# Linear attention over 32 heads: the last head's q work in halves, wide warm-up products, and new hand-written orders

## The chip, the cores and the metric

The kernel runs on one core of a Trainium2 chip. The metric is the time of one execution on the device, in microseconds (us). A core has a matrix engine (PE), a vector engine (DVE), a scalar engine (ACT), a general engine (POOL) and a sync engine (SP), which here only issues DMA transfers. Sixteen DMA engines carry the transfers.

## The reference

Every head has q, k and v of 2048 rows by 128 columns, in bf16.

```python
B, H, S, D = 1, 32, 2048, 128
phi_q = jnp.where(q > 0, q + 1, jnp.exp(q)) + 1e-6
phi_k = jnp.where(k > 0, k + 1, jnp.exp(k)) + 1e-6
kv  = jnp.einsum("bhsd,bhse->bhde", phi_k, v)
z   = jnp.einsum("bhsd->bhd", phi_k)
num = jnp.einsum("bhqd,bhde->bhqe", phi_q, kv)
den = jnp.einsum("bhqd,bhd->bhq", phi_q, z)[..., None] + 1e-6
return num / den
```

The feature map is computed as min(exp(x), 1) + 1e-6 plus max(x, 0). The two parts go through the products separately and are added in the accumulator.

## The kernel before

A head's 2048 rows are 16 tiles of 128 rows. The work of head h is cut into named operations, and each name carries the head and a part number:

- `ldk`, `ldq`, `ldv`: loads of 512 KB on SP's queue (line 300). Head 0's are two halves of 256 KB. There are 7 buffers for each of k, q and v (`NI`), so a load waits until the head 7 before has used its buffer.
- `ek` (ACT, line 312): exp of k. `em` (DVE, line 315): min and add. `rkd` (DVE, line 318) and `rkp` (POOL, line 322): max(k, 0), eight tiles each. `v1` (POOL, line 326): copies v beside a column of ones, so that z comes out of the same product.
- `kv` (PE, line 333): 32 products into one accumulator, in two halves of 16. `kvs` (ACT, line 338) copies the result to bf16.
- `T` (PE, line 344): 16 transposes of q into the one buffer `xT`. `eq` (ACT, line 347): exp of `xT`. `emq` (DVE, line 349): min and add. `rqa` (ACT, line 353) and `rqb` (DVE, line 356): max(q, 0), eight tiles each.
- `n` (PE, lines 363, 368 and 370): the numerator and denominator products, in two groups (12 and 4 tiles; for head 31 three groups of 6, 6 and 4). `r` (DVE, line 377): reciprocal of the denominators. `f` (DVE, line 384): the final product into one of 12 output buffers (`NO`).
- `st` (SP, line 392): the store, 512 KB; head 31's goes in pieces of 192, 192 and 128 KB. `f` of head h waits for the store of head h - 12.
- `w0`, `w1`, `w2` (PE, line 291): products on the identity matrix that nobody reads. They keep PE busy at the start.

Every engine runs its operations in the order that `ORDER` writes out by hand; a semaphore wait is put in wherever an operation needs another engine's result. So an operation that waits holds all that stands behind it on its engine, and a load or store that waits holds all later ones on SP. Waits that matter here: T of a head waits for `eq`, `rqa` and `rqb` of the head before, since `xT` is one buffer; `eq` waits for the `n` of the head two before; `n` of a group waits until `f` of the head before has emptied its banks. `rkp` and `v1` also wait for `f` and `r` of the head three before (`gate`). A half operation waits only for the halves that it touches:

```python
def over(name, h, parts, t0, t1):
    return [f"{name}{h}.{i}" for i, (a, b) in enumerate(parts(h)) if a < t1 and t0 < b]
```

Of the kernel before, what the change touches and what calls it, by code (L numbers as in the profile page):

```python
# [8 lines left out]
ENGINES = ("PE", "DVE", "ACT", "POOL", "SP")  # L9
NH = 32  # L10
NI, NO, NE, NR, NV, NQ, NK = 7, 12, 2, 2, 2, 2, 2
WARM = (60, 15, 15)
HALVES = ((0, 8), (8, 16))
WHOLE = ((0, 16),)

# [2 lines left out]
    return HALVES if h == 0 else WHOLE  # L18


q_parts = v_parts = k_parts


def kv_parts(h):
# [29 lines left out]
def gate(name, h):  # L54
    if h < 3:
# [3 lines left out]

ORDER = {  # L60
    "PE": """
        w2 T0.1 T0.0 w1 w0 T1.0 kv0.0 kv0.1 n0.0 kv1.0 kv1.1 T2.0 n0.1 n1.0 kv2.0 kv2.1 T3.0 n1.1 kv3.0 kv3.1 n2.0
        T4.0 n2.1 kv4.0 kv4.1 n3.0 T5.0 n3.1 kv5.0 kv5.1 n4.0 T6.0 n4.1 kv6.0 kv6.1 n5.0 T7.0 n5.1 kv7.0 kv7.1 n6.0
        T8.0 n6.1 kv8.0 kv8.1 n7.0 T9.0 n7.1 kv9.0 kv9.1 n8.0 T10.0 n8.1 kv10.0 kv10.1 n9.0 T11.0 n9.1 kv11.0 kv11.1
        n10.0 T12.0 n10.1 kv12.0 kv12.1 n11.0 T13.0 n11.1 kv13.0 kv13.1 n12.0 T14.0 n12.1 kv14.0 kv14.1 n13.0 T15.0
# [1 line left out]
        kv18.1 n17.0 T19.0 n17.1 kv19.0 kv19.1 n18.0 T20.0 n18.1 kv20.0 kv20.1 n19.0 T21.0 n19.1 kv21.0 kv21.1 n20.0  # L67
        T22.0 n20.1 kv22.0 kv22.1 n21.0 T23.0 n21.1 kv23.0 kv23.1 n22.0 T24.0 n22.1 kv24.0 kv24.1 n23.0 T25.0 n23.1
        kv25.0 kv25.1 n24.0 T26.0 n24.1 kv26.0 kv26.1 n25.0 T27.0 n25.1 kv27.0 kv27.1 n26.0 T28.0 n26.1 kv28.0
        kv28.1 n27.0 T29.0 n27.1 kv29.0 kv29.1 n28.0 T30.0 n28.1 kv30.0 kv30.1 n29.0 T31.0 n29.1 kv31.0 kv31.1 n30.0  # L70
        n30.1 n31.0 n31.1 n31.2
    """,
    "DVE": """
        rkd0.0 ones v1ones0 emq0.1 rqb0 emq0.0 rkd1.0 em0.0 em0.1 v1ones1 eps0 eps1 em1.0 eps2 emq1.0 rqb1 r0.0 f0.0
        rkd3.0 rkd2.0 em2.0 em3.0 rqb2 emq2.0 r0.1 f0.1 r1.0 rkd4.0 f1.0 em4.0 rqb3 r1.1 rkd5.0 f1.1 r2.0 emq3.0
        f2.0 em5.0 rqb4 r2.1 rkd6.0 f2.1 r3.0 emq4.0 f3.0 em6.0 rqb5 r3.1 rkd7.0 f3.1 r4.0 emq5.0 f4.0 em7.0 rqb6
        r4.1 f4.1 r5.0 emq6.0 f5.0 em8.0 rqb7 r5.1 f5.1 rkd8.0 r6.0 emq7.0 f6.0 em9.0 rqb8 r6.1 f6.1 rkd10.0 rkd9.0
        r7.0 emq8.0 f7.0 rkd11.0 rqb9 r7.1 em10.0 f7.1 r8.0 emq9.0 f8.0 em11.0 rqb10 r8.1 f8.1 rkd12.0 r9.0 emq10.0
        f9.0 em12.0 r9.1 rqb11 f9.1 emq11.0 r10.0 rkd13.0 f10.0 em13.0 rqb12 r10.1 f10.1 rkd14.0 r11.0 emq12.0 f11.0
        em14.0 r11.1 rqb13 f11.1 rkd15.0 r12.0 emq13.0 f12.0 em15.0 r12.1 rqb14 f12.1 rkd16.0 r13.0 emq14.0 f13.0  # L80
        em16.0 r13.1 rqb15 f13.1 rkd17.0 r14.0 emq15.0 f14.0 em17.0 r14.1 rqb16 f14.1 rkd18.0 r15.0 emq16.0 f15.0
        em18.0 rqb17 r15.1 rkd19.0 f15.1 r16.0 emq17.0 f16.0 em19.0 rqb18 r16.1 rkd20.0 f16.1 r17.0 emq18.0 f17.0
        em20.0 rqb19 r17.1 rkd21.0 f17.1 r18.0 emq19.0 f18.0 em21.0 rqb20 r18.1 f18.1 rkd22.0 r19.0 emq20.0 f19.0
        em22.0 rqb21 r19.1 f19.1 rkd23.0 r20.0 emq21.0 f20.0 em23.0 rqb22 r20.1 rkd24.0 f20.1 r21.0 emq22.0 f21.0
# [132 lines left out]
def bass_standalone__linear_attn_elu__prompt_kernel(nc: bass.Bass, q: bass.AP, k: bass.AP, v: bass.AP, out: bass.AP):  # L217
# [4 lines left out]
    NC = D + 1  # L222
# [6 lines left out]
    with ExitStack() as es:  # L229
        names = [0]  # L230

        def alloc(make, shape, dt):
            names[0] += 1
            return es.enter_context(make(f"la_{names[0]}", shape, dt))
# [222 lines left out]
```

## Time and profile before

| | us |
|---|---|
| median of 4 runs | 173.5 (172.84 to 173.87) |
| the profiled execution, its own time | 173.3 |
| its span in the profile | 171.4 |
| ACT busy in it | 153.3 |
| PE busy in it | 161.5 |
| DVE busy in it | 155.2 |

Times in the trace count from the start of the span. The line numbers are those of the kernel before. `PEld` is PE's load of the stationary operand, which overlaps its products. A DMA is told by the time from its issue on SP to its landing; it has landed when all 16 DMA engines have finished their part of it. The page cuts the span in 40 slices of 4.3 us; a digit is the busy share in tenths.

### The profile page before, as it was taken

To read this page: it belongs to the slowest core of one execution; us is meant where nothing else is said; L and a number is where in the kernel's file an instruction comes from. 1 tells how busy PE (TensorE), PEld (TensorE's weight loads), DVE (VectorE), ACT (ScalarE), POOL (GpSimd) and SP (SyncE) were. 2 spreads that over 40 slices of the span, in tenths; PEclk is the share of its full clock that TensorE was granted. 3 is DMA by queue.
4 is the path that set the end of the run, shared out by engine and by line. 5 is a ranking of instruction groups with operands and counts; after the bars stand their busy time and mean duration, and the time that the engine had idled before them with its cause. 6 is when DMAs were issued, how large, how long until landed. Compare 5 with 4: busy or idle time off the path is not lost.

```text
span 171.4 us, 6462 instructions
## 1 busy us (share of the span) xinstructions
PE 161.5 (94%) x2842; PEld 158.9 (93%) x2842; DVE 155.2 (91%) x266; ACT 153.3 (89%) x131; POOL 85.2 (50%) x71
## 2 busy tenths in 40 slices
PE   3997999999999999999999999999999999999771
PEld 3997989999999999999999999999999999999770
DVE  0539979999999999999999999999999999999883
ACT  2698799999999999999999999999999999996600
POOL 1255545556654565555665556655555555463000
PEclk9999999999999999999999999999999999999978
DMA  5999999999999999999999999999999999999883
GB/s 160 380 403 414 412 403 404 410 404 420 410 412 407 409 420 410 415 408 404 418 410 410 410 410 419 408 408 418 415 415 420 413 420 414 415 417 416 335 326 135
DMA packets 19180, 67.52 MB, mean 394 GB/s; under 512 B 2129, under 2 KB 2513, under 8 KB 19153
## 3 DMA queue, kind: packets, MB, share of 16 engines
q1 hardware_dynamic: 19152, 67.12, 97.9%
q8 instruction: 22, 0.36, 0.8%
q14 instruction: 6, 0.04, 0.1%
HBM read 50.33 MB, written 16.78 MB: 392 GB/s over the span
## 4 chain that ended last, share of the span: by engine, by line
ACT 58%; PE 29%; DVE 8%; DMA 2%; issue 2%; SPq 0%; DVEq 0%
ACT la L347 23%; ACT la L312 22%; ACT la L353 10%; PE la L333 10%; PE la L368 7%; PE la L370 6%; PE la L344 5%; DVE la L384 4%; ACT la L338 3%; DMA la<-in_q_dram 2%; DVE la L356 1%; DVE la L349 1%; DVE la L315 1%; PE la L363 1%; DVE la L377 1%
## 5 line engine op out<-in xcount | busy, mean ns | idle before, releaser
L384 DVE TENSOR_TENSOR la<-la 128x1536 bf16<-128x1536 f32 (+2 forms) x65 | 77.7, 1197 | 0.7
L370 PE MATMUL la<-la 128*128 128x129 bf16 x512 | 69.3, 222 | 0.0
L368 PE MATMUL la<-la 128*128 128x129 bf16 x512 | 69.2, 221 | 0.0
L347 ACT ACTIVATE la<-la 128x2048 bf16<-128x2048 bf16 (+1 forms) x33 | 60.1, 1825 | 5.9 <-PE la L344 3.7
L333 PE MATMUL la<-la 128*128 128x129 bf16 x1024 | 64.2, 219 | 0.4 <-DVE la L281 0.4
L312 ACT ACTIVATE la<-la 128x2048 bf16<-128x2048 bf16 (+1 forms) x33 | 61.2, 1861 | 0.0
L326 POOL COPY la<-la 128x1024 int32<-128x1024 int32 (+1 forms) x33 | 40.6, 1232 | 41.1 <-DVE la L377 34.7
L333 PEld LDWEIGHTS la<-la 128*128 128x128 bf16 x1024 | 60.1, 97 | 0.6 <-DVE la L281 0.6
L322 POOL TENSOR_SCALAR la<-la 128x1024 bf16<-128x1024 bf16 x32 | 43.9, 1371 | 29.4 <-DVE la L384 24.0
L370 PEld LDWEIGHTS la<-la 128*128 128x128 bf16 x512 | 50.0, 98 | 0.0
L368 PEld LDWEIGHTS la<-la 128*128 128x128 bf16 x512 | 47.7, 98 | 0.0
L344 PE MATMUL la<-la 128*128 128x128 bf16 x512 | 34.6, 222 | 1.6 <-DMA la<-in_q_dram 1.4
L363 PE MATMUL la<-la 128*128 128x3 bf16 (+1 forms) x192 | 32.5, 170 | 2.6 <-DVE la L384 1.9
L353 ACT ACTIVATE la<-la 128x1024 bf16<-128x1024 bf16 x32 | 32.6, 1018 | 0.0
L344 PEld LDWEIGHTS la<-la 128*128 128x128 bf16 x512 | 30.0, 99 | 2.3 <-DMA la<-in_q_dram 1.6
L315 DVE TENSOR_SCALAR la<-la 128x2048 bf16<-128x2048 bf16 (+1 forms) x33 | 23.2, 704 | 2.8 <-ACT la L312 2.8
L356 DVE TENSOR_SCALAR la<-la 128x1024 bf16<-128x1024 bf16 x32 | 21.8, 680 | 2.0 <-ACT la L347 1.3
L349 DVE TENSOR_SCALAR la<-la 128x2048 bf16<-128x2048 bf16 (+1 forms) x33 | 22.2, 672 | 1.4 <-ACT la L347 1.3
L363 PEld LDWEIGHTS la<-la 128*128 128x128 bf16 x192 | 18.9, 99 | 4.1 <-DVE la L384 2.8
L318 DVE TENSOR_SCALAR la<-la 128x1024 bf16<-128x1024 bf16 x32 | 14.2, 448 | 5.3 <-DMA la<-in_k_dram 5.3
L377 DVE RECIPROCAL la<-la 128x12 f32<-128x12 f32 (+2 forms) x65 | 12.8, 198 | 1.3 <-PE la L370 0.6
L338 ACT ACTIVATE la<-la 128x129 bf16<-128x129 f32 x32 | 9.0, 281 | 1.4 <-PE la L333 1.4
(14 smaller groups left out, 15.4 us busy)
## 6 DMA issues: line engine op xcount, KB each, us to landing
la<-in_k_dram SPq DMA_DIRECT2D x31, 512.0 KB, 15.6
la<-in_q_dram SPq DMA_DIRECT2D x31, 512.0 KB, 15.5
la<-in_v_dram SPq DMA_DIRECT2D x31, 512.0 KB, 15.3
out_dram<-la SPq DMA_DIRECT2D x31, 512.0 KB, 15.1
la<-in_q_dram SPq DMA_DIRECT2D x2, 256.0 KB, 3.0
la<-in_k_dram SPq DMA_DIRECT2D x2, 256.0 KB, 4.0
la<-in_v_dram SPq DMA_DIRECT2D x2, 256.0 KB, 6.3
out_dram<-la SPq DMA_DIRECT2D x2, 192.0 KB, 2.2
```

The costliest lines, as they stand in the source:

```text
L312: add("ACT", f"ek{h}.{i}", lambda e, a=a, b=b: e.activation(em_sb[:, h % NE, a:b], k_sb[:, h % NI, a:b], ACT.Exp), [f"ldk{h}.{i}"] + freed ...
L315: add("DVE", f"em{h}.{i}", lambda e, a=a, b=b: e.tensor_scalar(em_sb[:, h % NE, a:b], em_sb[:, h % NE, a:b], 1.0, EPS, op0=ALU.min, op1=AL ...
L322: add("POOL", f"rkp{h}.{i}", lambda e, a=a, b=b: e.tensor_scalar(rk_sb[:, h % NR, a:b], k_sb[:, h % NI, a:b], BIG, 0.0, op0=ALU.min, op1=A ...
L326: add("POOL", f"v1{h}.{i}", lambda e, a=a, b=b: e.tensor_copy(v1_sb[:, h % NV, a:b, 0:D].bitcast(i32), v_sb[:, h % NI, a:b].bitcast(i32)), ...
L333: ins = e.matmul(kv_ps, lhsT=src[:, j], rhs=v1_sb[:, h % NV, j, 0:NC], start=(j + part == 0), stop=(j == NT - 1 and part == 1))
L344: ins = e.transpose(xT[:, j], q_sb[:, h % NI, j], ident[:])
L347: add("ACT", f"eq{h}.{i}", lambda e, a=a, b=b: e.activation(emq_sb[:, h % NQ, a:b], xT[:, a:b], ACT.Exp), [f"T{h}.{i}"] + freed(NQ, h, ("n ...
L353: add("ACT", f"rqa{h}", lambda e: e.activation(rq_sb[:, h % NQ, 0:n], xT[:, 0:n], ACT.Relu), over("T", h, q_parts, 0, n) + freed(NQ, h, (" ...
L363: e.matmul(_ap(o_ps[:, :], o + D, [[NC, m]]), lhsT=ones[:], rhs=epsr[:, 0:m], start=True, stop=False, skip_group_check=True)
L368: e.matmul(to, lhsT=emq_sb[:, h % NQ, t], rhs=kvs_sb[:, h % NK], start=False, stop=False, skip_group_check=True)
L370: ins = e.matmul(to, lhsT=rq_sb[:, h % NQ, t], rhs=kvs_sb[:, h % NK], start=False, stop=True, skip_group_check=True)
L384: return e.tensor_tensor(out=_ap(o_sb[:, :, :, :], first(o_sb[:, h % NO, t0, 0:1]) - first(o_sb[:, :, :, :]), [[m * D, nb], [D, m], [1, D] ...
```

## The change

- q of head 31 is loaded, transposed and put through exp and min in two halves, as head 0's is. T31.1 comes first, then n29.1, then T31.0.
- The warm-up products become 480 columns wide, and there are 15, 4 and 4 of them instead of 60, 15 and 15. Their moving operand is the same 120 columns read four times.
- The orders of DVE, SP and of the starts and ends of the others are written anew. No operation is added or dropped but for the halves. The places named later are in the lines below.

```diff
-WARM = (60, 15, 15)
+WARM = (15, 4, 4)
...
-q_parts = v_parts = k_parts
+v_parts = k_parts
+
+
+def q_parts(h):
+    return HALVES if h in (0, NH - 1) else WHOLE
...
     "PE": """
-        w2 T0.1 T0.0 w1 w0 T1.0 kv0.0 kv0.1 n0.0 kv1.0 kv1.1 T2.0 n0.1 n1.0 kv2.0 kv2.1 T3.0 n1.1 kv3.0 kv3.1 n2.0
+        w2 T0.0 T0.1 w0 w1 T1.0 kv0.0 kv0.1 n0.0 kv1.0 kv1.1 T2.0 n0.1 n1.0 kv2.0 kv2.1 T3.0 n1.1 kv3.0 kv3.1 n2.0
...
-        kv28.1 n27.0 T29.0 n27.1 kv29.0 kv29.1 n28.0 T30.0 n28.1 kv30.0 kv30.1 n29.0 T31.0 n29.1 kv31.0 kv31.1 n30.0
-        n30.1 n31.0 n31.1 n31.2
+        kv28.1 n27.0 T29.0 n27.1 kv29.0 kv29.1 n28.0 T30.0 n28.1 kv30.0 kv30.1 n29.0 T31.1 n29.1 T31.0 kv31.0 kv31.1
+        n30.0 n30.1 n31.0 n31.1 n31.2
...
     "DVE": """
-        rkd0.0 ones v1ones0 emq0.1 rqb0 emq0.0 rkd1.0 em0.0 em0.1 v1ones1 eps0 eps1 em1.0 eps2 emq1.0 rqb1 r0.0 f0.0
+        eps0 v1ones1 v1ones0 eps1 emq0.0 rkd0.0 eps2 rkd1.0 rqb0 em0.0 em0.1 emq0.1 ones em1.0 emq1.0 rqb1 r0.0
...
-        em14.0 r11.1 rqb13 f11.1 rkd15.0 r12.0 emq13.0 f12.0 em15.0 r12.1 rqb14 f12.1 rkd16.0 r13.0 emq14.0 f13.0
+        emq12.0 f11.0 em14.0 r11.1 rqb13 f11.1 emq13.0 r12.0 rkd15.0 f12.0 em15.0 rqb14 r12.1 rkd16.0 f12.1 r13.0
...
-        rqb29 r27.1 emq29.0 f27.1 r28.0 em30.0 f28.0 em31.0 rqb30 r28.1 f28.1 r29.0 rkd31.0 f29.0 emq30.0 emq31.0
-        rqb31 r29.1 r30.0 f29.1 f30.0 r30.1 f30.1 r31.0 f31.0 r31.1 f31.1 r31.2 f31.2
+        f27.0 em30.0 rqb29 r27.1 f27.1 rkd30.0 r28.0 emq29.0 f28.0 em31.0 rqb30 r28.1 f28.1 r29.0 rkd31.0 f29.0
+        emq30.0 rqb31 emq31.0 r29.1 f29.1 r30.0 f30.0 emq31.1 r30.1 f30.1 r31.0 f31.0 r31.1 f31.1 r31.2 f31.2
...
     "ACT": """
-        eq0.1 eq0.0 rqa0 ek0.0 ek1.0 ek0.1 eq1.0 kvs0 rqa1 ek2.0 kvs1 ek3.0 eq2.0 rqa2 kvs2 ek4.0 eq3.0 kvs3 rqa3
+        eq0.0 rqa0 eq0.1 ek0.0 ek0.1 ek1.0 eq1.0 kvs0 rqa1 ek2.0 kvs1 ek3.0 eq2.0 rqa2 kvs2 ek4.0 eq3.0 kvs3 rqa3
...
-        ek26.0 eq25.0 kvs25 rqa25 ek27.0 eq26.0 kvs26 rqa26 ek28.0 eq27.0 kvs27 rqa27 ek29.0 eq28.0 rqa28 kvs28
-        ek30.0 eq29.0 kvs29 rqa29 ek31.0 eq30.0 kvs30 rqa30 eq31.0 rqa31 kvs31
+        ek26.0 eq25.0 kvs25 rqa25 ek27.0 eq26.0 kvs26 rqa26 ek28.0 eq27.0 kvs27 rqa27 ek29.0 eq28.0 kvs28 rqa28
+        ek30.0 eq29.0 kvs29 rqa29 ek31.0 eq30.0 kvs30 rqa30 eq31.1 eq31.0 kvs31 rqa31
...
     "POOL": """
-        ident0 ident rkp0.0 v10.0 v10.1 v11.0 rkp1.0 rkp2.0 v12.0 rkp3.0 v13.0 v14.0 rkp4.0 v15.0 rkp5.0 v16.0
+        ident0 ident v10.0 rkp0.0 v10.1 v11.0 rkp1.0 rkp2.0 v12.0 rkp3.0 v13.0 v14.0 rkp4.0 v15.0 rkp5.0 v16.0
...
     "SP": """
-        ldq0.0 ldq0.1 ldk0.0 ldk0.1 ldk1.0 ldq1.0 ldv0.0 ldv0.1 ldv1.0 ldk2.0 ldq2.0 ldk3.0 ldv2.0 ldq3.0 ldk4.0
+        ldq0.0 ldq0.1 ldk0.0 ldk0.1 ldk1.0 ldv0.0 ldq1.0 ldv0.1 ldv1.0 ldk2.0 ldq2.0 ldk3.0 ldv2.0 ldq3.0 ldk4.0
...
-        ldq16.0 ldv16.0 ldv17.0 ldv18.0 ldk18.0 ldq17.0 ldk19.0 ldq18.0 st5.0 ldv19.0 ldk20.0 ldk21.0 ldq19.0
-        ldq20.0 ldv20.0 ldv21.0 ldv22.0 ldv23.0 ldk22.0 st6.0 st7.0 st8.0 ldk23.0 ldq21.0 ldk24.0 ldq22.0 ldk25.0
+        ldq16.0 ldk17.0 ldq17.0 st3.0 ldq18.0 ldk18.0 ldq19.0 ldk19.0 st4.0 ldv18.0 ldk20.0 ldk21.0 ldk22.0 ldv19.0
+        ldk23.0 st5.0 ldq20.0 st6.0 ldv20.0 ldv21.0 st7.0 ldq21.0 st8.0 ldq22.0 ldv22.0 ldq23.0 ldv23.0 st9.0
...
-        ldk28.0 ldk29.0 ldq27.0 st13.0 ldv28.0 st14.0 ldk30.0 ldq28.0 ldv29.0 ldq29.0 ldq30.0 st15.0 ldv30.0 ldv31.0
-        ldk31.0 ldq31.0 st16.0 st17.0 st18.0 st19.0 st20.0 st21.0 st22.0 st23.0 st24.0 st25.0 st26.0 st27.0 st28.0
-        st29.0 st30.0 st31.0 st31.1 st31.2
+        st13.0 ldv27.0 ldq27.0 ldq28.0 ldv28.0 ldk29.0 st14.0 ldq29.0 ldv29.0 st15.0 ldq30.0 ldq31.0 ldk30.0 ldv30.0
+        ldk31.0 ldq31.1 st16.0 ldv31.0 st17.0 st18.0 st19.0 st20.0 st21.0 st22.0 st23.0 st24.0 st25.0 st26.0 st27.0
+        st28.0 st29.0 st30.0 st31.0 st31.1 st31.2
...
         def warm(key, n):
             def g(e):
                 for w in range(n):
-                    ins = e.matmul(o_ps[:, 512 + 3 * NC:512 + 3 * NC + 120], lhsT=ident[:], rhs=ident[:, 0:120],
+                    ins = e.matmul(o_ps[:, 512:992], lhsT=ident[:], rhs=_ap(ident[:, :], 0, [[0, 4], [1, 120]]),
                                    start=(w == 0), stop=(w == n - 1))
```

More of the change, by code (lines that the diff above doesn't have):

```diff
@@ L75 @@
[L75 to L79, printed above, removed]
@@ L80 @@
-        em14.0 r11.1 rqb13 f11.1 rkd15.0 r12.0 emq13.0 f12.0 em15.0 r12.1 rqb14 f12.1 rkd16.0 r13.0 emq14.0 f13.0
[L81 to L84, printed above, removed]
@@ L85 @@
-        em24.0 r21.1 rqb23 f21.1 emq23.0 r22.0 rkd25.0 f22.0 em25.0 rqb24 r22.1 f22.1 rkd26.0 emq24.0 r23.0 f23.0
-        em26.0 r23.1 rqb25 f23.1 emq25.0 r24.0 rkd27.0 f24.0 em27.0 rqb26 r24.1 f24.1 emq26.0 r25.0 f25.0 em28.0
-        rqb27 r25.1 f25.1 rkd29.0 r26.0 rkd28.0 f26.0 emq27.0 rqb28 em29.0 r26.1 f26.1 r27.0 rkd30.0 f27.0 emq28.0
-        rqb29 r27.1 emq29.0 f27.1 r28.0 em30.0 f28.0 em31.0 rqb30 r28.1 f28.1 r29.0 rkd31.0 f29.0 emq30.0 emq31.0
-        rqb31 r29.1 r30.0 f29.1 f30.0 r30.1 f30.1 r31.0 f31.0 r31.1 f31.1 r31.2 f31.2
+        eps0 v1ones1 v1ones0 eps1 emq0.0 rkd0.0 eps2 rkd1.0 rqb0 em0.0 em0.1 emq0.1 ones em1.0 emq1.0 rqb1 r0.0
@@ new lines @@
+        rkd2.0 f0.0 em2.0 rkd3.0 em3.0 rqb2 emq2.0 r0.1 f0.1 r1.0 rkd4.0 f1.0 em4.0 rqb3 r1.1 rkd5.0 f1.1 r2.0
+        emq3.0 f2.0 em5.0 rqb4 r2.1 rkd6.0 f2.1 r3.0 emq4.0 f3.0 em6.0 r3.1 rqb5 f3.1 rkd7.0 r4.0 emq5.0 f4.0 em7.0
+        r4.1 rqb6 f4.1 rkd8.0 r5.0 emq6.0 f5.0 em8.0 rqb7 r5.1 f5.1 rkd9.0 r6.0 emq7.0 f6.0 em9.0 r6.1 rqb8 f6.1
+        rkd10.0 r7.0 emq8.0 f7.0 em10.0 rqb9 r7.1 f7.1 emq9.0 r8.0 rkd11.0 f8.0 em11.0 r8.1 rqb10 f8.1 emq10.0 r9.0
+        rkd12.0 f9.0 em12.0 rqb11 r9.1 f9.1 emq11.0 r10.0 rkd13.0 f10.0 em13.0 r10.1 rqb12 f10.1 rkd14.0 r11.0
@@ new lines @@
+        emq12.0 f11.0 em14.0 r11.1 rqb13 f11.1 emq13.0 r12.0 rkd15.0 f12.0 em15.0 rqb14 r12.1 rkd16.0 f12.1 r13.0
+        emq14.0 f13.0 em16.0 rqb15 r13.1 rkd17.0 f13.1 r14.0 emq15.0 f14.0 em17.0 rqb16 r14.1 rkd18.0 f14.1 r15.0
+        emq16.0 f15.0 em18.0 r15.1 rqb17 rkd19.0 f15.1 r16.0 emq17.0 f16.0 em19.0 r16.1 rqb18 rkd20.0 f16.1 r17.0
+        emq18.0 f17.0 em20.0 rqb19 r17.1 rkd21.0 f17.1 r18.0 emq19.0 f18.0 em21.0 r18.1 rqb20 f18.1 emq20.0 r19.0
+        rkd22.0 f19.0 em22.0 r19.1 rqb21 rkd23.0 f19.1 r20.0 emq21.0 f20.0 em23.0 r20.1 rqb22 f20.1 rkd24.0 r21.0
@@ new lines @@
+        emq22.0 f21.0 em24.0 rqb23 r21.1 f21.1 rkd25.0 r22.0 emq23.0 f22.0 em25.0 r22.1 rqb24 f22.1 rkd26.0 r23.0
+        emq24.0 f23.0 em26.0 rqb25 r23.1 rkd27.0 f23.1 r24.0 emq25.0 f24.0 em27.0 rqb26 r24.1 f24.1 r25.0 emq26.0
+        f25.0 em28.0 rqb27 r25.1 rkd28.0 f25.1 r26.0 emq27.0 f26.0 em29.0 rqb28 r26.1 emq28.0 f26.1 r27.0 rkd29.0
+        f27.0 em30.0 rqb29 r27.1 f27.1 rkd30.0 r28.0 emq29.0 f28.0 em31.0 rqb30 r28.1 f28.1 r29.0 rkd31.0 f29.0
+        emq30.0 rqb31 emq31.0 r29.1 f29.1 r30.0 f30.0 emq31.1 r30.1 f30.1 r31.0 f31.0 r31.1 f31.1 r31.2 f31.2
@@ L108 @@
     "SP": """
-        ldq0.0 ldq0.1 ldk0.0 ldk0.1 ldk1.0 ldq1.0 ldv0.0 ldv0.1 ldv1.0 ldk2.0 ldq2.0 ldk3.0 ldv2.0 ldq3.0 ldk4.0
-        ldv3.0 ldv4.0 ldq4.0 ldk5.0 ldv5.0 ldv6.0 ldq5.0 ldk6.0 ldk7.0 ldv7.0 ldk8.0 ldq6.0 ldk9.0 ldv8.0 ldq7.0
-        ldq8.0 st0.0 ldk10.0 ldq9.0 st1.0 ldv9.0 ldv10.0 ldv11.0 ldq10.0 ldk11.0 ldk12.0 ldk13.0 ldv12.0 ldv13.0
-        ldq11.0 st2.0 ldq12.0 st3.0 ldq13.0 ldq14.0 ldk14.0 ldv14.0 ldk15.0 ldv15.0 st4.0 ldk16.0 ldq15.0 ldk17.0
-        ldq16.0 ldv16.0 ldv17.0 ldv18.0 ldk18.0 ldq17.0 ldk19.0 ldq18.0 st5.0 ldv19.0 ldk20.0 ldk21.0 ldq19.0
-        ldq20.0 ldv20.0 ldv21.0 ldv22.0 ldv23.0 ldk22.0 st6.0 st7.0 st8.0 ldk23.0 ldq21.0 ldk24.0 ldq22.0 ldk25.0
-        ldv24.0 ldk26.0 ldq23.0 ldq24.0 ldk27.0 st9.0 ldv25.0 st10.0 ldq25.0 ldv26.0 st11.0 ldq26.0 ldv27.0 st12.0
-        ldk28.0 ldk29.0 ldq27.0 st13.0 ldv28.0 st14.0 ldk30.0 ldq28.0 ldv29.0 ldq29.0 ldq30.0 st15.0 ldv30.0 ldv31.0
-        ldk31.0 ldq31.0 st16.0 st17.0 st18.0 st19.0 st20.0 st21.0 st22.0 st23.0 st24.0 st25.0 st26.0 st27.0 st28.0
-        st29.0 st30.0 st31.0 st31.1 st31.2
+        ldq0.0 ldq0.1 ldk0.0 ldk0.1 ldk1.0 ldv0.0 ldq1.0 ldv0.1 ldv1.0 ldk2.0 ldq2.0 ldk3.0 ldv2.0 ldq3.0 ldk4.0
+        ldv3.0 ldv4.0 ldk5.0 ldq4.0 ldv5.0 ldq5.0 ldk6.0 ldq6.0 ldv6.0 ldv7.0 ldq7.0 ldk7.0 ldv8.0 ldk8.0 st0.0
+        ldq8.0 ldk9.0 ldq9.0 ldk10.0 ldq10.0 ldv9.0 st1.0 ldv10.0 ldk11.0 ldv11.0 ldk12.0 ldq11.0 ldv12.0 ldv13.0
+        ldv14.0 ldq12.0 ldq13.0 ldk13.0 st2.0 ldk14.0 ldk15.0 ldv15.0 ldv16.0 ldv17.0 ldq14.0 ldk16.0 ldq15.0
+        ldq16.0 ldk17.0 ldq17.0 st3.0 ldq18.0 ldk18.0 ldq19.0 ldk19.0 st4.0 ldv18.0 ldk20.0 ldk21.0 ldk22.0 ldv19.0
+        ldk23.0 st5.0 ldq20.0 st6.0 ldv20.0 ldv21.0 st7.0 ldq21.0 st8.0 ldq22.0 ldv22.0 ldq23.0 ldv23.0 st9.0
+        ldq24.0 ldq25.0 ldk24.0 ldq26.0 ldv24.0 st10.0 ldk25.0 ldv25.0 ldk26.0 ldv26.0 st11.0 st12.0 ldk27.0 ldk28.0
+        st13.0 ldv27.0 ldq27.0 ldq28.0 ldv28.0 ldk29.0 st14.0 ldq29.0 ldv29.0 st15.0 ldq30.0 ldq31.0 ldk30.0 ldv30.0
+        ldk31.0 ldq31.1 st16.0 ldv31.0 st17.0 st18.0 st19.0 st20.0 st21.0 st22.0 st23.0 st24.0 st25.0 st26.0 st27.0
+        st28.0 st29.0 st30.0 st31.0 st31.1 st31.2
     """,
```

## The prediction

> **What bounds the kernel now.** I read the page first, then the chain, then the stores one by one. Sections 1 to 3 of the page:
>
> ```profile
> PE 161.5 (94%) x2842; PEld 158.9 (93%) x2842; DVE 155.2 (91%) x266; ACT 153.3 (89%) x131; POOL 85.2 (50%) x71
> ...
> PEclk9999999999999999999999999999999999999978
> DMA  5999999999999999999999999999999999999883
> GB/s 160 380 403 414 412 403 404 410 404 420 410 412 407 409 420 410 415 408 404 418 410 410 410 410 419 408 408 418 415 415 420 413 420 414 415 417 416 335 326 135
> ...
> q1 hardware_dynamic: 19152, 67.12, 97.9%
> ```
>
> Four things are full at once: PE, DVE, ACT and the 16 DMA engines (67.12 MB at some 412 GB/s). The chain of waits, in order of time, goes through compute:
>
> ```profile
> 1.17 3.41 DMA la<-in_q_dram
> 4.63 1.05 PE la L344 x8
> 5.70 1.94 ACT la L347 x2
> ...
> 8.55 3.69 ACT la L312 x3
> 12.27 0.99 DVE la L315
> ...
> 158.38 1.89 ACT la L347
> ```
>
> By this view compute is the bound: ACT starts at 5.70, takes some 4.72 us a head (1.80 + 1.78 + 0.91 + 0.24) and is never idle for long until 156.6. But look at the stores at the end (each line pair is one store: issue time, then time to landing), and at the DMA share there:
>
> ```profile
> L392 SPq DMA_DIRECT2D out_dram<-la x1: 332/332/332, 152.7 to 152.7; - x1
> ...
> DMA to landing us min/median/max: 12.2/12.2/12.2
> ...
> L392 SPq DMA_DIRECT2D out_dram<-la x1: 333/333/333, 157.2 to 157.2; - x1
> ...
> DMA to landing us min/median/max: 9.0/9.0/9.0
> ...
> L392 SPq DMA_DIRECT2D out_dram<-la x1: 333/333/333, 162.5 to 162.5; - x1
> ...
> DMA to landing us min/median/max: 4.9/4.9/4.9
> ...
> L392 SPq DMA_DIRECT2D out_dram<-la x1: 332/332/332, 165.0 to 165.0; - x1
> ...
> DMA to landing us min/median/max: 3.7/3.7/3.7
> ```
>
> ```profile
> 160.00:163.00 3.00, 2.13 (x42) 1.95 (x39) 2.70 (x6) 1.35 (x3) 0.00 (x0) 1.00 0.73 292
> 163.00:167.00 4.00, 3.02 (x38) 2.84 (x36) 3.25 (x6) 0.00 (x0) 0.00 (x0) 0.71 0.82 333
> ```
>
> st27 to st30 are issued 4.5, 5.3 and 2.5 us apart, yet land at 164.9, 166.2, 167.4 and 168.7: 1.25 us apart, the pace of a full queue. A store lands when the slowest of its 16 engines is done. So, although the mean DMA share falls to 0.73 after 160, one engine has a backlog until 168.7. The three pieces of st31 land at 169.1, 169.9 and 170.65 (issued 166.6, 168.0, 168.8); only the last two, with 1.9 and 1.85 us to landing, wait for compute. The span ends 0.73 us later, at 171.4; the run took 173.3, which is 1.9 more, and 0.2 under the median of 173.5.
>
> **The start.** T0.1 went first and waited for the second load (1.17 + 3.41 = 4.58). T0.0 needs the first, issued at 0.74 and landed 2.6 us later, at 3.35. eq0.0 can start at about 4.5 instead of 5.70. The same 6.4 us of ACT work then lead to eq1.0: 10.9 instead of 12.12. With ek0.1 before ek1.0, em0.1 no longer waits until 12.24, so kv0.1 can follow kv0.0; that gap was 0.4 us. v0.0 moves before q1 on SP: it lands 1.3 us sooner (8.3), q1 0.63 later (9.6). POOL now holds rkp0.0 behind v10.0: 8.3 + 0.77 + 1.03 = 10.1, which no kv waits for.
>
> The warm-ups keep their columns: 75 x 120 = 9,000 for w0 and w1 become 19 x 480 = 9,120. Before, a 120-column product took 0.101 us until 7.74 and 0.054 after it, so 480 columns are about 0.40 and 0.214. From 5.5 that is 5.5 slow and 13.5 fast ones: they end at 10.6, where T1.0 started at 10.94. The Trainium skill (TensorE: Matmul & The Clock Gate, Part 4: PE-mode transpose) says that transposes do not count as activity for the clock. By it T0.0's earlier start would leave the clock at half until 7.74. The trace speaks against it: the clock rose at 7.74 after 3.1 us that were half transposes, though 1.7 us of products before 3.2 had not raised it. By the trace the clock may rise as early as 4.3, the warm-ups end at 9.6, and T1.0 is 0.9 earlier still. I keep both ends: T1.0 at 9.7 to 10.6; kv0.1 ends 2.96 later, kvs0 at 13.0 to 13.9, n0.0 at 13.1 to 14.0 instead of 14.88. **Gain 0.9 to 1.8.**
>
> **The middle.** ACT's order is the same but for kvs28 and rqa28. DVE's moves by a place or two; ACT was idle only 0.4 us between 20 and 150, and DVE 3.0. So at most 0.4 is to be won; a late emq would cost ACT what DVE's 3.0 does not cover. I take 0. On SP the loads and stores change places. I set each new place against the landing time of that place in the queue before. Most slacks stay over 2 us, but k30 goes from 103 units of 512 KB to 108.5 and would land at 145.6, and ek30 started at 146.60. So ACT cannot be over 1.0 us ahead there. Nor does the queue run dry: the nearest case is ldk23 (place 78 to 69), free to go when rkp16 ends, at 85.3, while the fastest engine has work until 89.7. st5, which is behind it, lands at 96, and f17, which needs it, started at 100.9.
>
> **The tail.** eq31 waited for n29.1, which ran behind all 16 transposes of T31. With T31.1 alone ahead, n29.1 is 8 x 0.057 = 0.46 earlier, and eq31.1 starts at 157.9 instead of 158.38. kvs31 now goes before rqa31 and waits for kv31 (160.2), which brings rqa31 back to 161.3; n31.0 doesn't need it that early. Halving costs 0.06 on ACT (2 x 0.97 for 1.88) and 0.1 on DVE. DVE from 159.14: emq30 0.61, rqb31 0.61, emq31.0 0.36, r29.1 and f29.1 0.8 end at 161.5 (was 162.45); n30.0 ends at 161.65; f30.0 at 163.5 (164.1); emq31.1, r30.1, f30.1 at 164.7; three r and f of 1.1, 1.1 and 0.87: f31.2 ends at 167.8 instead of 168.77. If PE falls to half clock as before (0.11 a product from 164.7), n31.0 is late by 0.4. **Gain 0.6 to 1.0.** Compute in all: at most 1.0 at ek30 and 0.6 to 1.0 behind it, about 1.5 to 2.0 us.
>
> **The DMA floor.** Bytes and first issue are the same, so the slowest engine has the same work. It can land st30 at 168.65 at the earliest, and st31 (192 + 192 + 128 KB) is one store more: 1.25 us at the pace above, and 0.49 for its first 192 KB as measured. If compute delivers in time, the last piece lands at 169.9 instead of 170.65: 0.75 us less. q31 as two 256 KB loads adds 0.1 to 0.2 (halves at the start took about 0.7 to 0.8 on the median engine, against 1.28 for a whole one). Compute needs f31.2 by 168.0 for this, and has it by 166.8 to 167.3. So of 1.5 to 2.0 us only 0.75 less 0.1, **about 0.7**, reaches the end: 173.3 - 0.7 = 172.6, or 172.8 against the median. I say 172.7. The Trainium skill (DMA: Bandwidth & Descriptors, Anatomy of one DMA) gives 2.0 us + bytes / 436 GB/s: 156 us by that, 14 us of slack, and the whole compute gain would show (171.3 to 171.8). The trace measured 412 GB/s and an engine that is still behind at 168.7, so it decides.
>
> **Rivals.** *Compute was the bound after all:* the slowest engine loses its lag, or other loads delay it less; then 1.5 to 2.0, and 2.5 if k30 lands early: 171.0 to 171.8. For it: the chain. Against it: the 1.25 us rhythm. 13%. *Nothing arrives:* the halves and one more delay on the slowest engine (landings there jumped by about 1 us three times, at 21, 80 and 134) eat the 0.7: 173.2 to 174. 13%. *k30 becomes the wait:* its slack falls from 7.8 to 1.0 us. Each us of later landing holds ek30, and ACT, already full, passes it on to f31.2 undiminished. Compute has about 2 us to lose against before, so it decides from a landing past 148.7; at 150.5 it costs about 1.8: 175.3. For it: ldk30 now stands behind both ldq31.0 and st15. Against it: a queue that never runs dry. 14%. The floor holds the remaining 60%, with 172.2 to 173.2 as its own range.
>
> **The numbers.** About 0.5% (0.87 us) is what a measurement of this kernel can tell. The floor lies just at that edge, so I split it 28 to 32. Faster: 13 + 28 = 41%; same: 32 + 13 = 45%; slower: 14%. The range of 171.5 to 174.2 leaves out most of the first and the last rival.
>
> **What would show it.** First transposes at 3.4; n0.0 near 13.5; f31.2 about 1.5 us earlier; st27 to st31.2 landing in one unbroken 1.25 us rhythm (by their sizes), with the last near 169.9; DMA share near 1 until the landings end only on some engines. I am wrong if the last stores land 1.8 us after issue with no backlog, if ACT waits for a k load near 146, or if the DMA row has a gap before 155.

## The result, and the profile after

| | before | after |
|---|---|---|
| median | 173.26 us (64 runs, 172.23 to 173.96) | 172.78 us (43 runs, 171.76 to 173.95) |
| ratio of the times | | 0.9973 (95%: 0.9961 to 0.9985) |
| span of the profiled execution | 171.4 | 171.0 |
| f31.2, the last DVE operation, ends | 168.77 | 168.20 |
| last landing | 170.65 | 170.25 |

The change gains 0.3%, about 0.5 us. The forecast was 172.7. The same kernel was measured twice more, each time beside new runs of the kernel before: 0.9965 and 0.9955. The ratios are taken over all runs but one slow one (175.02 us, of start alone); they are not the quotients of the medians shown beside them.

The page of the changed kernel, sections 1 to 3. The engines are as full as before, by the same bytes; PE's clock now has a dip in the third and fourth slice.

```profile
PE 160.1 (94%) x2775; PEld 155.2 (91%) x2775; DVE 153.6 (90%) x267; ACT 153.3 (90%) x132; POOL 85.8 (50%) x71
...
PEclk9987999999999999999999999999999999999997
DMA  5999999999999999999999999999999999999975
GB/s 182 305 390 416 410 409 407 411 410 411 414 413 407 407 412 415 406 406 419 410 424 405 416 419 412 416 414 415 419 413 422 411 413 419 413 415 415 368 301 206
...
q1 hardware_dynamic: 19296, 67.12, 98.3%
q8 instruction: 22, 0.36, 0.8%
```

The last stores of the changed kernel, one line pair each as before (issue, then time to landing): st27, st28, st29, st30 and the last piece of st31.

```profile
L396 SPq DMA_DIRECT2D out_dram<-la x1: 332/332/332, 152.8 to 152.8; - x1
...
DMA to landing us min/median/max: 12.4/12.4/12.4
...
L396 SPq DMA_DIRECT2D out_dram<-la x1: 332/332/332, 157.5 to 157.5; - x1
...
DMA to landing us min/median/max: 8.9/8.9/8.9
...
L396 SPq DMA_DIRECT2D out_dram<-la x1: 333/333/333, 161.9 to 161.9; - x1
...
DMA to landing us min/median/max: 5.7/5.7/5.7
...
L396 SPq DMA_DIRECT2D out_dram<-la x1: 333/333/333, 165.2 to 165.2; - x1
...
DMA to landing us min/median/max: 3.7/3.7/3.7
...
L396 SPq DMA_DIRECT2D out_dram<-la x1: 332/332/332, 168.2 to 168.2; - x1
...
DMA to landing us min/median/max: 2.0/2.0/2.0
```

They land at 165.2, 166.4, 167.7, 168.9 and 170.25: one unbroken rhythm of about 1.25 us up to the end. The last store's 2.0 us are 0.2 over the shortest seen (1.85 in the kernel before), so in this execution compute and the slowest DMA engine end almost together. The windows at the end (stretch, length, busy time of PE, PEld, DVE, ACT and POOL, granted clock, DMA share, GB/s) show that the mean over 16 engines hides this: it is at 0.82 and 0.76 while at least one engine still has a queue.

```profile
160.00:163.00 3.00, 2.64 (x48) 2.31 (x44) 2.82 (x7) 1.41 (x3) 0.00 (x0) 1.00 0.82 333
163.00:167.00 4.00, 2.15 (x38) 1.98 (x38) 3.90 (x8) 0.00 (x0) 0.00 (x0) 1.00 0.76 301
```

The start is not what was forecast. The chain of waits, in order of time (start, length, what):

```profile
3.52 7.48 DMA la<-in_q_dram
...
11.13 1.63 PE la L348 x16
12.76 2.89 PE la L337 x32
...
15.67 0.29 ACT la L342
```

q1 landed at 11.0 instead of the forecast 9.6. T1.0 waited for it, and n0.0 began at 16.10: 1.22 us later than before, where 0.9 to 1.8 us earlier was expected. The windows show the second loss, behind the first:

```profile
8.94:11.13 2.19, 0.00 (x0) 0.03 (x1) 2.02 (x4) 2.19 (x2) 1.36 (x2) 1.00 1.01 369
11.13:15.00 3.87, 3.87 (x40) 3.87 (x41) 2.36 (x5) 1.89 (x2) 2.71 (x4) 0.56 1.03 418
```

The warm-ups ended at 8.94, PE was idle for 2.19 us, and the granted clock then fell to half from 11.42 to 14.84. So kv0 took 2.89 us; kv1 a little later took 1.85. Compute nevertheless ended 0.57 us earlier than before, so over 1.7 us were won behind n0.0. Where these come from, and why so little of it reaches the end, is what the experiments ask.

### The profile page after: what moved, and what is told of

It reads as the page before. It is cut to its first block, busy times and chain, and to the rows that moved or that the text cites. A ratio compares the mean times of both kernels' runs of the same rounds, so it can differ in the third digit from the quotient of the medians.

```text
span 171.0 us, 6324 instructions
## 1 busy us (share of the span) xinstructions
PE 160.1 (94%) x2775; PEld 155.2 (91%) x2775; DVE 153.6 (90%) x267; ACT 153.3 (90%) x132; POOL 85.8 (50%) x71
## 4 chain that ended last, share of the span: by engine, by line
PE 84%; DVE 5%; DMA 4%; ACT 2%; SPq 1%; issue 1%
PE la L337 34%; PE la L372 18%; PE la L348 16%; PE la L374 16%; DMA la<-in_q_dram 4%; DVE la L388 3%; SPq L304 1%; ACT la L316 1%; ACT la L351 1%; PE la L367 1%; DVE la L353 1%; DVE la L381 1%; DVE la L360 0%; ACT la L342 0%
## 5 line engine op out<-in xcount | busy, mean ns | idle before, releaser
L353 DVE TENSOR_SCALAR la<-la 128x2048 bf16<-128x2048 bf16 (+1 forms) x34 | 21.5, 632 | 6.2 <-ACT la L351 6.2
L319 DVE TENSOR_SCALAR la<-la 128x2048 bf16<-128x2048 bf16 (+1 forms) x33 | 23.2, 704 | 0.0
L322 DVE TENSOR_SCALAR la<-la 128x1024 bf16<-128x1024 bf16 x32 | 14.4, 450 | 2.6 <-DMA la<-in_k_dram 2.6
## 6 DMA issues: line engine op xcount, KB each, us to landing
out_dram<-la SPq DMA_DIRECT2D x31, 512.0 KB, 14.8
```

What stands on the lines that cost most here:

```text
L353: add("DVE", f"emq{h}.{i}", lambda e, a=a, b=b: e.tensor_scalar(emq_sb[:, h % NQ, a:b], emq_sb[:, h % NQ, a:b], 1.0, EPS, op0=ALU.min, op1 ...
```

## The experiments

Two theories. **Floor:** the slowest DMA engine sets the end, whatever compute wins. **Compute:** the chain of ACT, PE and DVE sets it, and the gain is small because the start went wrong. Ratios are to the kernel before, measured on the same chip, with 95% intervals.

### Taking compute away, taking bytes away, and both

Compute of two late heads halved (from `after`; `cu` halves the tiles of exp, min, transposes, products and max(q, 0), and a shorter `groups` those of the final product; max(k, 0), the copy of v, loads and stores stay):

```diff
+CUT = (29, 30)
...
+            cu = 2 if h in CUT else 1
...
-                    em_sb[:, h % NE, a:b], k_sb[:, h % NI, a:b], ACT.Exp),
+                    em_sb[:, h % NE, a:b // cu], k_sb[:, h % NI, a:b // cu], ACT.Exp),
...
-                    for j in range(a, b):
+                    for j in range(a // cu, b // cu):
```

> The changed kernel with the compute of heads 29 and 30 halved on PE, ACT and DVE (it leaves out half of their exp, transposes, products and final products); all loads and stores stay. By the widths, ACT, PE and DVE lose some 3 us before f31.2 (168.2 in the changed kernel), and f31.2 comes near 165. Floor theory (the slowest DMA engine sets the end): the stores of heads 27 to 31 still land 1.25 us apart, the last near 170, and the time falls by 0 to 0.4 us against the changed kernel, so 172.3 to 172.8, ratio to before 0.995 to 0.998. Compute theory (the chain through ACT, PE and DVE is the bound): some 3 us less, 169.8, ratio near 0.980.

Stores of four heads taken away (from `after`), and the same together with the cut:

```diff
-        ... st19.0 st20.0 st21.0 st22.0 st23.0 st24.0 ...
+        ... st19.0 st24.0 ...
```

> The changed kernel without the stores of heads 20 to 23 (it leaves these outputs out): 2.1 MB or 5.0 us less for the DMA engines, compute as it is. Floor theory, with compute close behind the floor: the DMA queue is empty by 165, f31.2 stays near 168.2, the last store lands 1.85 us after its issue, near 170.1, and the time falls by 0.1 to 0.3 us: 172.5. A theory in which DMA alone sets the time: 5.0 us less, 167.8. Compute theory: no change, 172.8.

> Both edits at once: half the compute of heads 29 and 30, and no stores of heads 20 to 23. Floor theory: neither edit alone brings more than 0.4 us, both together bring what the later of the two leaves, some 3 us: 169.8, ratio near 0.980. Compute theory: the same 3 us, but then the halved compute alone must already have brought them. DMA alone: 5 us, as without the stores alone.

The changed kernel once more, unedited, beside them:

> The changed kernel as it is, for a second profile. In its first one the second half of k0 landed at 7.83 on its last DMA engine (6.41 before the change), q1 at 11.0, PE idled from 8.94 to 11.13, its clock fell to half until 14.84, and n0.0 started at 16.10 instead of 14.88. If this belongs to the change (order of the loads, narrower gaps), it comes again, with n0.0 near 16. If it is chance on the DMA engines, q1 lands near 9.6 and n0.0 starts at 13.1 to 14.0. The end differs little by the floor theory (last store near 170, 172.8) and by over 2 us by the compute theory.

| kernel | median us | ratio | f31.2 ends | st30 lands | last landing |
|---|---|---|---|---|---|
| after, again | 172.5 | 0.9965 (0.9946 to 0.9984) | 166.78 | 169.09 | 170.42 |
| compute cut | 172.45 | 0.9959 (0.9938 to 0.9981) | 162.83 | 168.56 | 169.90 |
| four stores less | 171.41 | 0.9900 (0.9856 to 0.9943) | 167.32 | 168.23 | 169.44 |
| both | 168.75 | 0.9739 (0.9697 to 0.9781) | 164.47 | 165.06 | 166.42 |

With compute cut, its last store is issued at 162.9, four us earlier, and lands at 169.9, within what the other profiles of these bytes show (169.07 to 170.80). The store, and then the windows of that kernel:

```profile
L400 SPq DMA_DIRECT2D out_dram<-la x1: 332/332/332, 162.9 to 162.9; - x1
...
DMA to landing us min/median/max: 7.0/7.0/7.0
```

```profile
160.00:163.00 3.00, 0.94 (x19) 0.77 (x16) 2.76 (x5) 0.00 (x0) 0.00 (x0) 1.00 1.02 414
163.00:166.00 3.00, 0.00 (x0) 0.00 (x0) 0.00 (x0) 0.00 (x0) 0.00 (x0) 0.78 0.88 350
166.00:168.00 2.00, 0.00 (x0) 0.00 (x0) 0.00 (x0) 0.00 (x0) 0.00 (x0) 0.50 0.57 224
```

From 163 on no engine computes at all; for 7 us the DMA engines run dry one after another. That is the floor, bare. With four stores less the queue at the end is nearly gone: the last stores of that kernel land 2.1 to 3.9 us after issue, and the share of the DMA engines is 0.4.

```profile
L395 SPq DMA_DIRECT2D out_dram<-la x5: 332/332/996, 161.1 to 167.4; - x5
...
DMA to landing us min/median/max: 2.1/2.6/3.9
```

```profile
160.00:163.00 3.00, 1.77 (x32) 1.44 (x28) 2.82 (x5) 0.88 (x1) 0.00 (x0) 1.00 0.42 169
163.00:167.00 4.00, 2.15 (x38) 1.98 (x38) 3.86 (x10) 0.00 (x0) 0.00 (x0) 1.00 0.41 152
```

Against `after, again`, the cut alone gives 0.05 us (uncertain by about 0.5, as the two intervals have it), the stores alone 1.09, both together 3.75: three times the sum. Two limits lie close together, and each hides what is taken from the other. Their sizes fit: the changed kernel's floor is 169.9 on average and its compute ends at 168.7 (both worked out below), so fewer stores can give 1.2 until compute is the limit; the cut takes 2.6 to 3.1 us between n0.0 and f31.2, which both together add to it. Of the stores alone I had expected 0.2 us and of both together some 3 us (169.8, against 168.75), and missed both. The estimates were built on f31.2 at 168.20 in the first profile of the changed kernel, which has a late start; the kernel usually ends compute earlier (166.78 here, 165.57 in a third profile), and so leaves more room above it.

### Adding bytes

Two loads of 512 KB that nobody reads, put late into SP's queue (from `after`), and the changed kernel again beside it:

```diff
-        ... st16.0 ldv31.0 st17.0 ...
+        ... st16.0 ldv31.0 x0 x1 st17.0 ...
```

> The changed kernel with two more loads of 512 KB (k of head 0 once more, into tiles that nobody reads), put between ldv31.0 and st17.0: 1.05 MB or 2.5 us more for every DMA engine, compute untouched; f29 needs st17 only at 157, and it would land at 155.3. Floor theory: the last stores land 2.5 us later, and the time rises by all of it: 175.1, ratio to before near 1.011. Compute theory: nothing waits for these loads, no change, 0.997.

> The changed kernel once more, on the same chip as the next one. Ratio to before 0.995 to 0.998, as in its two measurements (0.9973 and 0.9965).

175.2 us, 1.0112 (1.0082 to 1.0143), against 172.5 us, 0.9955 (0.9939 to 0.9970) for the changed kernel beside it. So 1 MB costs 2.7 us, which is all of its time in a full queue (2 x 1.25 = 2.5). Nothing of it is hidden. Its f31.2 ended at 166.07, so the loads did not hold compute; its last landing came at 172.23. The profile of the changed kernel's repeat shows the floor where compute is early. Its stores st28, st29, st30 and the last piece of st31:

```profile
L396 SPq DMA_DIRECT2D out_dram<-la x1: 332/332/332, 154.9 to 154.9; - x1
...
DMA to landing us min/median/max: 10.9/10.9/10.9
...
L396 SPq DMA_DIRECT2D out_dram<-la x1: 332/332/332, 159.3 to 159.3; - x1
...
DMA to landing us min/median/max: 7.7/7.7/7.7
...
L396 SPq DMA_DIRECT2D out_dram<-la x1: 332/332/332, 162.6 to 162.6; - x1
...
DMA to landing us min/median/max: 5.7/5.7/5.7
...
L396 SPq DMA_DIRECT2D out_dram<-la x1: 332/332/332, 165.6 to 165.6; - x1
...
DMA to landing us min/median/max: 4.0/4.0/4.0
```

Compute is 2.6 us earlier than in the first profile of the changed kernel (165.57 against 168.20), the last landing only 0.7 (169.59 against 170.25), and the last store now waits 4.0 us instead of 2.0.

### The parts of the change one by one

Start alone (from `before`: PE, ACT, POOL and SP as in the change's first lines, DVE's new order up to emq2.0, the wide warm-ups):

```diff
-WARM = (60, 15, 15)
+WARM = (15, 4, 4)
...
-        w2 T0.1 T0.0 w1 w0 T1.0
+        w2 T0.0 T0.1 w0 w1 T1.0
...
-        eq0.1 eq0.0 rqa0 ek0.0 ek1.0 ek0.1
+        eq0.0 rqa0 eq0.1 ek0.0 ek0.1 ek1.0
...
-        ldq1.0 ldv0.0
+        ldv0.0 ldq1.0
```

> The kernel before with the start of the change alone: 480-column warm-ups, T0.0, eq0.0 and v0.0 first, ek0.1 before ek1.0. In five profiles of the new start n0.0 began at 13.7 to 16.1 (14.88 before). The tail is the old one, with 1.85 us between f31.2 and the last landing that no queue fills, so here compute counts: a start that is 1 us early shows as 0.75 us or less, one that is 1 us late as 1 us. I expect no change within 0.3%: ratio 0.997 to 1.003. By the prediction's own step (n0.0 0.9 to 1.8 early) it would be 0.9957.

Tail alone (from `before`: q31 in halves and the last lines of PE, DVE and ACT):

```diff
-        n29.0 T31.0 n29.1
+        n29.0 T31.1 n29.1 T31.0
...
-        emq30.0 emq31.0 rqb31 r29.1 r30.0 f29.1 f30.0 r30.1
+        emq30.0 rqb31 emq31.0 r29.1 f29.1 r30.0 f30.0 emq31.1 r30.1
...
-        eq31.0 rqa31 kvs31
+        eq31.1 eq31.0 kvs31 rqa31
```

> The kernel before with the tail of the change alone: q of head 31 in halves, T31.1 n29.1 T31.0 on PE, and the new last orders of ACT and DVE; start, middle and SP's order stay. The tail took f31.2 from 16.6 us after the start of ek31 to 16.0 in the first profile of the change (17.17 to 16.01 us, a gain of 1.2). Floor theory: f31.2 near 167.6, the last store lands near 169.9 behind a queue, 0.5 to 0.75 us less than before: ratio 0.9957 to 0.997, all that the whole change brings. Compute theory: 1.2 us, ratio 0.993. If the start of the change is what brings its gain: no change here.

The kernel before, unedited, for a second profile:

> The kernel before, unchanged, for a second profile. It tells chance from cause at the start: if k0.1 lands on its last engine near 6.4 again, the later landing (7.5 to 8.4) belongs to the new start; if it lands between 6.4 and 8.4 it is chance. The last stores should again land 1.25 us apart from st27 to st30, and the last one 1.85 us after its issue.

Middle alone (from `before`: DVE's new order between emq2.0 and emq30.0, SP's behind the start, and kvs28 ahead of rqa28; q31 stays whole):

```diff
-        ... eq28.0 rqa28 kvs28 ...
+        ... eq28.0 kvs28 rqa28 ...
...
-        rkd10.0 rkd9.0 r7.0 emq8.0 f7.0 rkd11.0 rqb9 r7.1 em10.0 f7.1
+        rkd10.0 r7.0 emq8.0 f7.0 em10.0 rqb9 r7.1 f7.1
```

> The kernel before with the middle of the change alone: the new orders of DVE between emq2 and emq30 and of SP after the start, kvs28 before rqa28; old start, old tail, q of head 31 whole. No compute is saved, f31.2 stays near 168.3 to 168.8. Floor theory and compute theory: no change, ratio 0.998 to 1.002. If it comes out near 0.996 to 0.997, the gain of the change sits in the DMA order, which neither theory says.

And the change without its start, twice, on two chips:

```diff
-WARM = (15, 4, 4)
+WARM = (60, 15, 15)
...
-        w2 T0.0 T0.1 w0 w1 T1.0
+        w2 T0.1 T0.0 w1 w0 T1.0
...
-        eq0.0 rqa0 eq0.1 ek0.0 ek0.1 ek1.0
+        eq0.1 eq0.0 rqa0 ek0.0 ek1.0 ek0.1
```

> The changed kernel with the start of the kernel before (its warm-ups, its first orders on all engines): the middle and the tail alone are new. Floor theory: again 0.995 to 0.997 of before, like the whole change. If the late last engine of k0.1 (7.5 to 8.4 in four of the five profiles of the new start, 6.41 in the one of before) comes from the new start, the floor itself falls by some 0.3 to 1 us: ratio 0.992 to 0.995, and this beats both. Compute theory: the start of the change moved n0.0 between -1.2 and +1.2 us, so undoing it moves the time as much the other way.

> The changed kernel with the old start once more, beside the changed kernel itself. It had 0.9950 with an interval that takes in the changed kernel's value. Floor theory: both have the same floor and differ by less than 0.15%, 0.995 to 0.998. If the old start is truly better for the DMA engines, it comes out near 0.995 again and the changed kernel near 0.997.

| kernel | median us | ratio |
|---|---|---|
| start alone | 172.63 | 0.9972 (0.9954 to 0.9989) |
| tail alone | 172.81 | 0.9972 (0.9954 to 0.9990) |
| middle alone | 172.39 | 0.9956 (0.9940 to 0.9972) |
| before, one run | 172.77 | |
| change without its start | 172.12 | 0.9950 (0.9932 to 0.9969) |
| the same, second chip | 172.26 | 0.9947 (0.9924 to 0.9970) |

Each part alone gives about what all three give together. Were compute the bound, they would add up to 1.0%. The change without its start looks best, but its 0.9947 stands beside 0.9955 for the whole change on the same chip, and the intervals cover each other; I cannot call it better.

Of the middle I had expected 0.998 to 1.002, and missed. The starts of ek and eq in the profiles tell why. They repeat to about 0.01 us between profiles of kernels that share a part. "Without its start" stands for both of its runs.

| stretch, us | before, twice | start alone | tail alone | middle alone | after, three times | without its start |
|---|---|---|---|---|---|---|
| ek10 to ek20 | 47.61, 47.60 | 47.61 | 47.60 | 47.25 | 47.25 | 47.25 |
| ek30 to ek31 | 5.00 | 5.00 | 5.00 | 4.72 | 4.73 | 4.73 |
| ek31 to the first eq31 | 6.79 | 6.79 | 6.34 | 6.54 | 6.09 | 6.09 |
| from there to the end of f31.2 | 10.39, 10.20 | 9.84 | 9.92 | 9.84 | 9.92 | 9.92 |

The middle takes 0.35 + 0.27 + 0.25 = 0.87 us out of compute: it removes three waits of ACT, at eq10 (0.25), eq29 (0.16) and eq30 (0.15). Two of them stand in the waits of the kernel before between 20 and 152 us (engine, line, what it waited for: us in all, times, longest):

```profile
ACT la L347 <- PE la L370: 0.4, 2, 0.2
```

The changed kernel and the middle alone have no ACT line in that view. The wait at eq29, between ek30 and ek31, in the two starts of the ek line, before and then after:

```profile
L312 ACT ACTIVATE la<-la x2: 1912/1917/1922, 146.6 to 151.6; 128x2048 bf16<-128x2048 bf16 x2
```

```profile
L316 ACT ACTIVATE la<-la x2: 1912/1912/1912, 147.5 to 152.2; 128x2048 bf16<-128x2048 bf16 x2
```

Each of the three cost 0.1 us more than its idle time, since two ACT instructions back to back overlap by 0.1 us in the trace (eq31.1 ends at 159.30, eq31.0 starts at 159.20) and a wait takes that overlap away too. So the middle alone saves 0.87 us of compute in an otherwise old kernel, and 0.76 us arrived (0.44% of 173.2; 0.48 to 1.04 by the interval). The new order of the loads and stores is part of this kernel too, and no run separates the two.

### One table for the end

What ends last in each profile: the DMA engines (the landing of st30 + 1.3 us for st31's 512 KB) or compute (the end of f31.2 + 1.87 us for a store's landing)? The last landing is the larger of the two, within 0.1 us, in every row. The 1.3 and the 1.87 us are read from these same profiles, so the table is a summary; what decides are the edits above.

| profile | n0.0 starts | floor | compute | last landing |
|---|---|---|---|---|
| before | 14.88 | 169.94 | **170.64** | 170.65 |
| before, again | 14.57 | 169.13 | **170.14** | 170.14 |
| start alone | 13.58 | **169.94** | 168.96 | 169.96 |
| tail alone | 14.19 | **170.79** | 169.69 | 170.80 |
| middle alone | 15.21 | **170.29** | 169.58 | 170.26 |
| after | 16.10 | **170.22** | 170.07 | 170.25 |
| after, second | 14.71 | **170.39** | 168.65 | 170.42 |
| after, third | 13.31 | **169.56** | 167.44 | 169.59 |
| without its start | 15.20 | **169.35** | 169.18 | 169.34 |
| without its start, second | 14.87 | **169.06** | 168.83 | 169.07 |
| compute cut | 13.68 | **169.86** | 164.70 | 169.90 |
| four stores less | 14.79 | **169.53** | 169.19 | 169.44 |
| both | 15.02 | 166.36 | 166.34 | 166.42 |
| two loads more | 14.00 | **172.20** | 167.94 | 172.23 |

The kernel before is the only one with just its own bytes that ends with compute. In the other nine such rows, compute varies over 5.4 us (164.70 to 170.07) and the last landing over 1.7, and the two do not go together. With four stores less the two lie 0.3 us apart and the queue is nearly gone, and that profile is of the slowest of its four runs (172.05 us), so which of them ended it is not settled by the row.

## Why the prediction was right, step by step

**The floor: right.** The forecast put the last landing at 169.9. The mean of the floor column over the eleven rows that move the kernel's own bytes is 169.87. The cut decides between the floor and the chain of waits: its f31.2 ended 4 us earlier, and that gave 0.05 us. The trace also has a time for each of a DMA's 16 parts: with compute cut, the first part of st30 landed at 163.23 and the last at 168.56, so the slowest engine was 5 us behind the fastest. The forecast set 156 us by the Trainium skill beside its own (DMA: Bandwidth & Descriptors, Anatomy of one DMA). That was a misreading: the section's fit is for one DMA that POOL issues, while these are 134 in SP's queue, so it sets no bound here. The floor of a single profile is worth less than I made of it: it ranges over 1.7 us, and the 169.9 read from one execution was close to the mean by luck. What the two halves of q31 cost on the DMA engines (0.1 to 0.2 in the forecast) is smaller than that and was not separated.

**The start: the step that failed.** Expected was a gain of 0.9 to 1.8 us at n0.0. The eight profiles with the new start give 13.31 to 16.10 (mean 14.4), the six with the old 14.19 to 15.21 (mean 14.8). So the gain is 0.4 us on average, with an uncertainty as large, and between +1.6 and -1.2 in one run; four of the eight lie inside the forecast 13.1 to 14.0. The step from T1.0 to n0.0 was right: 3.4 us in seven of the eight.

The term that was mis-sized is q1's landing, 9.6, taken from one profile as if it were fixed. It came at 9.82 to 11.49 (mean 10.6), later in all eight. T1.0 started within 0.2 us of it in seven; in the second profile it waited for the warm-ups. q1's new place cost what was forecast: it landed 3.4 us after k0.1 on average, against 2.8 with the old order. But k0.1 itself landed between 6.16 and 8.35 with the new start, and between 6.17 and 7.61 with the old. The means are 7.2 and 6.5. Whether the new start adds to the delay or this is chance stays open: the second profile of the kernel before (6.20) speaks for the new start by what I had written down, tail alone with its old start (7.61) against it. Single packets near 5 us took 1.0 to 1.7 us instead of about 0.1 in late profiles, but also in middle alone, where k0.1 landed at 6.17, so they do not explain it.

The moment at which the clock rises was the other loose term. The Trainium skill (TensorE: Matmul & The Clock Gate, Part 1: The HAM clock gate) has the clock decided in free-running windows of 3.4 us; the half-clock stretch of 3.42 us above agrees with that length. The same page (Part 4: PE-mode transpose) says that transposes do not count as busy in the same way. The traces speak for the forecast's reading, that they count: in the kernel before, the window from 4.21 to 7.63 held 1.32 us of identity products and 1.89 of transposes, and the clock rose at its end (7.63 in the clock's own record; the forecast had read 7.74 off the products); the one before it held 1.71 us of products and no transposes, and it did not. In the second profile of the change without its start, 0.99 and 1.89 us were enough. But no rule comes out of this: in the changed kernel's second profile 1.06 and 2.07 us, from 2.55 to 5.97, were not enough, and the clock rose only at 9.38. With the new start it rose between 4.60 and 9.99 in the eight profiles. The products of the warm-up, in the first and then in the second profile (ns min/median/max, stretch):

```profile
L295 PE MATMUL la<-la x19: 366/366/366, 4.9 to 8.6; 128*128 128x480 bf16 x19
```

```profile
L295 PE MATMUL la<-la x12: 366/607/607, 5.7 to 9.7; 128*128 128x480 bf16 x12
```

The same 480 columns last 366 ns or 607 ns. My range for the rise should have been wider. In the first profile the early rise did no good: the warm-ups ended at 8.94, PE was idle before a late q1, and the half-clock stretch followed.

**The middle: too low.** Taken as 0, at most 0.4; measured 0.87. The 0.4 was the idle time of ACT up to 150 in the waits. Missing were the third wait, behind 150, and the 0.1 us of lost overlap at each. By luck it did not spoil the sum, since the start was too high by about as much.

**The tail: right in sum, with help from the clock.** Expected 0.6 to 1.0 us: 1.0 if the clock holds with the new tail, 0.6 if it falls as before. Of ek31 to f31.2's end, the kernel before took 17.18 and 16.99, the tail alone 16.26: 0.7 to 0.9. eq31.1 comes 0.45 earlier, as worked out. The rest, 0.3 to 0.5, is the clock: in both profiles of before it fell to half during n31 (164.6 and 164.5), with the new tail in none of ten before f31.2 ended. But the new tail need not be the reason: start alone and middle alone keep the old tail, held the clock past 168.6 as well, and have the last stretch 0.08 us shorter than the new tail. Against start alone (16.63) the new tail gains only 0.37 us, less than the 0.6 forecast for a like clock. Why the clock fell in the two profiles of before stays open.

**Compute in all: right by two errors.** 1.5 to 2.0 us were forecast. Mean ends of f31.2 are 168.52 before (two profiles) and 166.85 after (three): 1.7 us. With 1.87 for the last store's landing, after's compute ends at 168.7 on average. The gain that arrives, 0.5 to 0.8 us over the three measurements, fits the forecast 0.7.

**The rivals.** *Compute was the bound:* fallen with the cut. *Nothing arrives:* excluded by the interval, 0.9961 to 0.9985, though the gain stays within the 0.5% that I called measurable. *k30 becomes the wait:* it cost next to nothing, but its slack was used up. k30 landed at 145.87, 146.03 and 144.53 in the three profiles of the changed kernel (145.6 was forecast), and ek30 started at 147.46, 146.05 and 144.83. In the second it started 0.02 us after the landing, without a measurable wait of ACT; with compute cut and with two loads more it was as close, and ek30 came 0.03 to 0.06 us late. In the third profile ek7 waited 0.15 us for k7. So a start that is faster still would meet the loads.

## What to carry to other kernels

When the mean DMA share is near one for most of the span, read the last transfers one by one: here, landings at even steps behind uneven issues meant that a DMA engine had a queue, and then a shortcut in compute was worth only the distance between compute's end and that queue's end. Test such a pair of limits by taking from each alone and from both: effects that don't add up (0.05, 1.09, and 3.75 together) showed it here, and they also say that several good edits will pay for only one. And never take a landing time or the moment of a clock change from one profile: the engines' own stretches repeated to 0.01 us here, these two did not.

## What the runs showed of the hardware

- The slowest of the 16 DMA engines ends a run of the same bytes anywhere within 1.7 us (st30 lands between 167.76 and 169.49), with no relation to the order of the queue that these profiles show: mean 168.5 with the new order (seven profiles), 168.7 with the old (four). I had taken the lag as a property of the kernel.
- Instructions come by DMA too (the q8 line: 22 packets, 0.36 MB, 0.9 to 1.1 us each). They are probably PE's, which runs most of the instructions. In the kernel before, three jumps of about 1 us of the slowest engine fell together with such packets, at 21, 79 and 134 us. Whether they make the lag was not tried.
- The chain of waits of the changed kernel ascribes 84% of the span to PE and does not name the queue that ended it: by the landings above, that queue ran on to the end, and this view shows no wait for it.
